# The seam between a routed and a dense mixture of experts: branch moved, shared block finished later

## The chip, the cores and the metric

The kernel runs on one core of a Trainium2 chip. The metric is device time in microseconds of one execution. Times inside a profile count from the first instruction of the profiled execution. TensorE (PE) multiplies, with its weight loads in a row of their own (PEld); VectorE (DVE), ScalarE (ACT) and GpSimd (POOL) do the rest, and SyncE (SP) issues most transfers.

## The reference

Three stages follow each other. Attention with rotated positions gives 1152 rows of 512 values. Each row then goes to one of 8 experts (`_moe_ref`), and the result goes through 8 experts that all work on all rows (`_moe2_ref`), weighted by a normalised gate:

```python
def _moe_ref(x, expert_emb, tau, w1, w2):
    ...
    expert_idx = np.argmax(logits, axis=1)
    ...
    for e in range(E):
        mask = expert_idx == e
        h = np.maximum(x[mask] @ w1[e], 0.0)
        out[mask] = gate_w[mask, None] * (h @ w2[e])

def _moe2_ref(x, w_gate, w1, w2):
    logits = x @ w_gate
    P = np.exp(logits - logits.max())
    for _ in range(8):
        P /= P.sum(1, keepdims=True) + 1e-09
        P /= P.sum(0, keepdims=True) + 1e-09
        P *= N / E
    for e in range(E):
        ye = np.maximum(x @ w1[e], 0.0) @ w2[e]
        out += P[:, e:e + 1] * ye
```

Sizes are N = 1152 rows, DM = 512, F = 1024 hidden values and E = 8.

## The kernel before

**Routed experts.** Rows are sorted into blocks of 128 rows of one expert. `run_blocks` works off NS = 10 blocks in a loop over i; iteration i holds the first layer of block i (`block_l1`) and the second layer of block i - 1 (`block_l2`). Weights come in 512 KB pieces into four raw buffers per layer (`fetch`, left out by a condition when the next block has the same expert) and are split by ScalarE and VectorE into a high and a low part (`split`). `block_in` gathers a block's rows from DRAM (xd); `block_out` scales the result by the gate and GpSimd scatters its rows to DRAM (yd) with an indirect transfer.

**The shared block.** Experts with few rows left over share one more block, number NB: four groups of 32 rows, each with its own expert's weights. `place_quad` finds its rows, `quad_tokens` turns them, `quad_product(s)` for s = 0 to 3 is a quarter of its first layer, `quad_relu` and `quad_turn` follow, and s = 4 to 7 are quarters of its second layer. `quad_fetch(s)` loads the 2 MB of weights that product s needs. In the old kernel the eight products stand in iterations 3 to 9 and its rows are scattered like those of any block.

**The branch.** Data may need more than 10 blocks. `rest_of_blocks` does those, behind a branch on a count that every engine reads for itself (`tc.If`, line 1009). With the data timed here it is not taken. Its not-taken side lets each queue wait for its own outstanding work.

**Dense experts.** `dense_experts` is a generator that is stepped from `run_blocks` for its first weights (`fetch1`, `prep_plain`). Behind the branch it loads yd in four quarters of 288 rows (line 1188), turns them on TensorE (`turn_quarter`, with warming products on a weight tile ahead), splits them into high and low parts (`split_quarter`) and starts the products (`plain`), the gate's normalisation (`sinkhorn`) and then the steady loop of `l1` and `l2`.

TensorE, VectorE, ScalarE and GpSimd run in the order in which the code is written. SyncE's order is made by a scheduler; each engine works its queue in order.

Of the kernel before, what the change touches and what calls it, by code (L numbers as in the profile page):

```python
# [49 lines left out]
def fused_kernel(ctx, tc, qk, vv, tab, cst, emb, tau, w1a, w2a, wg, w1b, w2b, out):  # L50
# [37 lines left out]

    mctx = ExitStack()
    rt = mctx.enter_context(tc.tile_pool(name="rt", bufs=1))  # L90
    cs = rt.tile([128, C_END], F32, name="cs")
    uo = rt.tile([128, 256], BF16, name="uo")
    rt.tile([128, 8], F32, name="pad")

    raw1p, raw2p = ([rt.tile([128, 2, F], F32, name=f"raw{m}{i}") for i in range(2)] for m in (1, 2))
# [400 lines left out]
    def squares(b):  # L496
        for c in range(NQ):
            sq = tmp("sq", [QT, DM], BF16) if (b, c) == (0, 0) else ops["sq"]
            ops["sq"] = sq
            yield A.activation(sq, ops["x", b][:, c], AF.Square, accum_out=nsq[:, b, c:c + 1])  # L500

    gv = tmp("gv", [QT, 3, B, NQ, NB], BF16)
# [43 lines left out]
    def quad_slots():  # L546

        z = tmp("z", [QT, E])
        V.tensor_scalar(z, grp, float(GS), 1024.0, op0=ALU.mult, op1=ALU.add)
        V.scalar_tensor_tensor(z, inq, -1024.0, z, op0=ALU.mult, op1=ALU.add)  # L550
        V.tensor_tensor(ws, ohb[:, :, :NQ], z.unsqueeze(1).unsqueeze(1).to_broadcast([QT, B, NQ, E]), op=ALU.mult)
        V.tensor_reduce(blk, ws, axis=AX.X, op=ALU.add)
        V.tensor_tensor(blk, blk, rk, op=ALU.add)
        sl = [QT, B * NQ, BLK]
        V.tensor_tensor(slot.rearrange("p b t n -> p (b t) n"), over(col("iota"), 1, sl),
                        over(blk.rearrange("p b t -> p (b t)"), 2, sl), op=ALU.is_equal)
# [236 lines left out]

    def block_out(i, p):
        y = mp.tile([BLK, DM], F32, tag="y", bufs=2, name="y")
        A.activation(y, p, AF.Copy, scale=gate[:, i:i + 1])
        G.indirect_dma_start(out=yd, out_offset=bass.IndirectOffsetOnAxis(ap=idx[:, 1, i:i + 1], axis=0),
# [10 lines left out]
    def quad_fetch(s):  # L808
# [5 lines left out]
        for r in quad["reg"]:  # L814
            w = early.tile([128, F], F32, tag="w", bufs=8, name="qw")
# [43 lines left out]
    def rest_of_blocks():  # L859

        own = [nc.sync.value_load(bei[0:1, i:i + 1], min_val=0, max_val=E - 1) for i in range(NS, NB)]
        for n, i in enumerate(range(NS, NB)):
# [6 lines left out]
            x = mp.tile([128, F], F32, tag="qx", bufs=1, name="ex")  # L869
# [6 lines left out]
            h = block_relu(p)  # L876
            t = mp.tile([128, F], F32, tag="qx", bufs=1, name="eh")
# [5 lines left out]
            p = bank("y", 2, "y")  # L883
# [3 lines left out]
            block_out(i, p)  # L887

    def run_blocks(lo, hi, xb=None, w1=None, w2=None):

        def expert(i, raws, src, n):
            while len(reg) <= i < hi:
                reg.append(nc.sync.value_load(bei[0:1, len(reg):len(reg) + 1], min_val=0, max_val=E - 1))
            if 0 < i < hi:
                fetch(raws, src, n, reg[i], reg[i] != reg[i - 1])

        xb = xb or [block_in(i) for i in range(lo, min(lo + 2, hi))]
        if lo > 0:
            expert(lo, raw1, w1a, 128)
            expert(lo, raw2, w2a, 256)  # L900
        with tc.manual_schedule(engines=ORDERED):
            if w1 is None:
                *_, w1 = split(raw1p)
            expert(lo + 1, raw1, w1a, 128)
            if lo == 0:
                warm(w1[0][0], WARM)
            x = block_x(xb[0])
            if lo == 0:
                warm(w1[0][0], 3)
                split_low(raw2p[0], *w2[0])  # L910
            h = None
            for i in range(lo, hi + 1):
                begin, here, more = i == 0, i < hi, i + 1 < hi
# [10 lines left out]
                if i == 6:  # L924
                    quad_relu()
                elif i == 9:
                    block_out(NB, quad["p", 0])
                    tc.mark_branch_hint_location("rest", "LikelyTaken")
                if begin:
# [14 lines left out]
                if i in (6, 7):  # L944
                    quad_fetch(i - 1)
# [7 lines left out]
                if i + 2 < hi and len(xb) < i + 3 - lo:  # L953
# [3 lines left out]
                if more:  # L957
                    x = block_x(xb[i + 1 - lo])

                if i > lo:  # L960

                    turned = []
                    y = block_l2(h, w2, (lambda: turned.append(block_turn(hn))) if i == hi - 1 else None, i == hi)
                if i == 1:
                    place_rest(lambda: bank("x", 2, "gp"))
                    quad_slots()
                    quad_constants()
                elif i in (3, 4, 5, 7, 8):
                    quad_product({3: 0, 4: 1, 5: 2, 7: 5, 8: 6}[i])
                elif i == 6:  # L970
                    quad_turn()
# [3 lines left out]
                if i > lo:  # L975
                    block_out(i - 1, y)
                if here:
# [3 lines left out]
                    h = turned[0] if i == hi - 1 else block_turn(hn)  # L981
                if i in (1, 3, 4, 5, 7):
                    quad_fetch({1: 1, 3: 2, 4: 3, 5: 4, 7: 7}[i])
                for _ in range({7: 2, 9: 4}.get(i, 0)):
                    next(dense)

    reg = [0]
    with tc.manual_schedule(engines=ORDERED | {mybir.EngineType.SP}):
# [18 lines left out]
        dense = dense_experts(ctx, tc, early, yd, wgk, w1b, w2b, out, ident, ones)  # L1007
        run_blocks(0, NS, xb, pieces(first_w1), first_w2)
    with tc.If(nc.values_load(bei[0:1, NB:NB + 1], min_val=0, max_val=NB) > NS, label="rest"):
        rest_of_blocks()  # L1010
# [7 lines left out]
def dense_experts(ctx, tc, early, yd, wgk, w1b, w2b, out, ident, ones):  # L1018
# [124 lines left out]
    pp = ctx.enter_context(tc.tile_pool(name="pd", bufs=1, space=PSUM))  # L1143


# [33 lines left out]
    def htile():  # L1179

        return dp.tile([128, 2, 2, N], F32R, tag="h", bufs=2, name="h")

    gs = []
    for i in range(4):
        if i % 2 == 0:
            gt = dp.tile([128, 4 * N], F32, tag="h", bufs=2, name="g")
        g = gt[:TQ, i % 2 * 3 * DM:(i % 2 + 1) * 3 * DM].rearrange("p (t d) -> p t d", t=3)
        nc.sync.dma_start(out=g, in_=yd[i * QW:(i + 1) * QW].rearrange("(p t) d -> p t d", t=3))
        gs.append(g)
    for n in (2, 3):  # L1190
        fetch1(n)

    def turn_quarter(i, n):
# [3 lines left out]
        w = w1[0, 0]["t"][:, 0]  # L1197
        for _ in range(n):
            T.matmul(bank(d[0], 0), w[:, :128], w, start=True, stop=True)  # L1199
        for k in range(KD_):  # L1200
            for t in range(3):
                T.transpose(bank(d[k // 2], k % 2)[:, t:QW:3], gs[i][:, t, k * 128:(k + 1) * 128],  # L1202
                            ident[:TQ, :TQ])
        return d

# [105 lines left out]
    def plain(n, r, c, between=None):  # L1311
# [6 lines left out]
        for i, (a, y, k, wx, yx) in enumerate(todo):  # L1318
            if i and i % 3 == 0 and between:
                between(i)  # L1320
            for q in range(2):
                T.matmul(d[1][:, q, :QW], wv[:, wx, a, k], yq[yx][:, y, k, q * QW:(q + 1) * QW],  # L1322
                         start=(i == 0), stop=(i == len(todo) - 1))
# [27 lines left out]
    acc = dp.tile([128, N // 128, DM], F32, name="acc")  # L1351
# [194 lines left out]
```

## Time and profile before

| | |
|---|---|
| median of 3 runs | 1124.4 us (1123.49 to 1125.94) |
| the profiled execution | 1124.6 us, of which 1122.8 us lie between its first and last instruction (the span) |
| TensorE | busy 1095.6 us, 98% of the span |
| VectorE, ScalarE, GpSimd | 777.0, 467.6 and 130.6 us busy |
| mean granted clock of TensorE | 0.993 |
| chain of work that ended last | 67% TensorE, 1% VectorE in its named part |

In this execution attention ends around 172 us, the routed experts run to about 334 us, and the dense experts fill the rest. A busy TensorE in the profile is not one at its peak, since ends of products are modelled; what a stretch costs is read from the starts of what follows. "Idle before" in a row is the time in which the engine had nothing to do, with what ended it behind the arrow.

### The profile page before, as it was taken

To read this page: it belongs to the slowest core of one execution; us is meant where nothing else is said; L and a number is where in the kernel's file an instruction comes from. 1 tells how busy PE (TensorE), PEld (TensorE's weight loads), DVE (VectorE), ACT (ScalarE), POOL (GpSimd) and SP (SyncE) were. 2 spreads that over 40 slices of the span, in tenths; PEclk is the share of its full clock that TensorE was granted. 3 is DMA by queue.
4 is the path that set the end of the run, shared out by engine and by line. 5 is a ranking of instruction groups with operands and counts; after the bars stand their busy time and mean duration, and the time that the engine had idled before them with its cause. 6 is when DMAs were issued, how large, how long until landed. Compare 5 with 4: busy or idle time off the path is not lost.

```text
span 1122.8 us, 16884 instructions
## 1 busy us (share of the span) xinstructions
PE 1095.6 (98%) x6605; PEld 928.4 (83%) x6606; DVE 777.0 (69%) x1257; ACT 467.6 (42%) x742; POOL 130.6 (12%) x106
## 2 busy tenths in 40 slices
PE   8999996999989999999999999999999999999998
PEld 4777775777768989988988989899988989888987
DVE  6767768976753697867766667666676666766665
ACT  4656746776853433333333333223333233333330
POOL 7674403232220000000000000000000000000000
PEclk9999998999998999999999999999999999999999
DMA  8688713657725011111111111111111111111002
GB/s 243 181 226 261 183 28 128 244 198 262 242 90 159 22 60 52 38 38 54 41 57 38 39 40 55 57 39 38 38 58 53 41 38 39 57 40 55 20 1 85
DMA packets 74980, 102.09 MB, mean 91 GB/s; under 512 B 5128, under 2 KB 46600, under 8 KB 74128
## 3 DMA queue, kind: packets, MB, share of 16 engines
q1 hardware_dynamic: 72528, 94.12, 27.2%
q0 software_dynamic: 1760, 5.77, 1.4%
q8 instruction: 54, 0.88, 0.3%
q10 hardware_dynamic: 608, 1.07, 0.3%
q14 instruction: 30, 0.25, 0.1%
HBM read 110.31 MB, written 7.60 MB: 105 GB/s over the span
## 4 chain that ended last, share of the span: by engine, by line
PE 67%; DVE 1%; DMA 0%; issue 0%; SPq 0%
PE o L1359 35%; PE d L1305 29%; PE d L1322 2%; DMA g<-yd 0%; DVE acc L1365 0%; PE d L1202 0%; PE o L1249 0%; PE d L1199 0%; DVE h L1347 0%; DVE w L1071 0%; DVE w L1132 0%; PE o L1202 0%; DVE acc L1370 0%; DVE P L1284 0%; DVE rs L1273 0%
## 5 line engine op out<-in xcount | busy, mean ns | idle before, releaser
L1359 PE MATMUL o<-w,h 128*128 128x512 f32 x1728 | 435.6, 394 | 0.4 <-DVE acc L1365 0.4
L1305 PEld LDWEIGHTS d<-yq,w 128*128 128x128 f32 x2520 | 355.6, 188 | 17.9
L1305 PE MATMUL d<-yq,w 128*128 128x288 f32 x2520 | 367.3, 294 | 0.0
L1359 PEld LDWEIGHTS o<-w,h 128*128 128x128 f32 x1728 | 312.1, 188 | 57.8 <-DVE acc L1365 0.7
L1370 DVE SCALAR_TENSOR_TENSOR acc<-o,P,acc 128x512 f32<-128x512 f32 x252 | 189.1, 751 | 160.9 <-PE o L1359 160.9
L1346 ACT ACTIVATE h<-st 128x576 fp32r<-128x576 f32 x90 | 61.7, 685 | 217.3 <-DVE st L1336 217.3
L1333 ACT ACTIVATE st<-d 128x576 f32<-128x576 f32 x90 | 58.7, 652 | 219.3 <-PE d L1305 219.3
L725 DVE TENSOR_TENSOR wlo<-raw,whi 128x2048 fp32r<-128x2048 f32 x40 | 91.0, 2288 | 24.8 <-ACT whi L732 24.6
L1336 DVE TENSOR_TENSOR st<-st,d 128x576 f32<-128x576 f32 x90 | 67.6, 751 | 39.4 <-PE d L1305 39.4
L249 DVE TENSOR_REDUCE nb<-s 120x1 f32<-120x576 f32 (+1 forms) x80 | 60.3, 754 | 37.4 <-PE s L243 24.1
L1070 ACT ACTIVATE w<-raw 128x512 fp32r<-128x512 f32 x124 | 70.8, 574 | 19.6 <-DVE raw L1115 16.0
L255 ACT ACTIVATE p<-s,nb 120x576 f32<-120x576 f32 (+1 forms) x80 | 59.0, 737 | 47.0 <-DVE nb L249 44.6
L1071 DVE TENSOR_TENSOR w<-raw,w 128x512 fp32r<-128x512 f32 x124 | 76.5, 619 | 0.0
L732 ACT ACTIVATE whi<-raw 128x2048 fp32r<-128x2048 f32 x36 | 69.0, 1916 | 15.8 <-PE h L760 7.2
L1347 DVE SCALAR_TENSOR_TENSOR h<-st,h 128x576 fp32r<-128x576 f32 x90 | 67.5, 750 | 0.4 <-ACT h L1346 0.3
L243 PE MATMUL s<-kd,qd 128*120 128x288 f32 x280 | 54.5, 317 | 1.2 <-ACT p L255 1.2
L243 PEld LDWEIGHTS s<-kd,qd 128*120 128x120 f32 x280 | 38.5, 178 | 14.0 <-ACT ph L281 5.7
L300 PE MATMUL o<-ph,vr 120*64 120x288 f32 x320 | 46.8, 417 | 0.0
L283 DVE COPY ph<-pt 120x480 f32<-120x480 f32 x64 | 41.4, 648 | 2.1 <-PE pt L277 2.1
L1347 DVE SCALAR_TENSOR_TENSOR h<-d,h 128x576 fp32r<-128x576 f32 x38 | 28.7, 756 | 19.4 <-ACT h L1346 19.4
L1132 DVE TENSOR_TENSOR w<-raw,w 128x1024 fp32r<-128x1024 f32 x32 | 39.0, 1218 | 0.4 <-ACT w L1131 0.4
L277 PE MATMUL pt<-io,p 120*120 120x120 f32 x256 | 37.0, 267 | 1.2 <-DVE ph L283 1.2
(285 smaller groups left out, 1046.5 us busy)
## 6 DMA issues: line engine op xcount, KB each, us to landing
raw<-w1a SPq DMA_DIRECT2D x40, 512.0 KB
raw<-w2a SPq DMA_DIRECT2D x40, 512.0 KB
raw<-w1b SPq DMA_DIRECT2D x64, 256.0 KB
raw<-w2b SPq DMA_DIRECT2D x32, 512.0 KB
qw<-w1a SPq DMA_DIRECT2D x16, 512.0 KB
qw<-w2a SPq DMA_DIRECT2D x16, 512.0 KB
kd<-hl SPq DMA_DIRECT2D x28, 288.0 KB
r<-qk SPq DMA_DIRECT2D x6, 1152.0 KB
```

What stands on the lines that cost most here:

```text
L243: T.matmul(s[:m, h, :HS], qd[:, j, t * QT:t * QT + m], kd[:, j, x, h * HS:(h + 1) * HS], start=(x == 0), stop=(x == 1))
L249: V.tensor_reduce(nb[:m], s[:m, :, :HS], axis=AX.XY, op=ALU.max, negate=True)
L725: V.tensor_tensor(lo, raw, hi, op=ALU.subtract)
L732: A.activation(hi, raw, AF.Copy)
L1070: A.activation(hi, src, Copy)
L1071: V.tensor_tensor(lo, src, hi, op=ALU.subtract)
L1305: T.matmul(d[1][:, q, :QW], wv[:, wx, which, k], yq[yx][:, YQ[p], k, q * QW:(q + 1) * QW], start=new and k == 0 and (wx, yx) == (0, 0), st ...
L1336: V.tensor_tensor(halves(st[x]), halves(st[x]), mid(d), op=ALU.add)
L1346: A.activation(hi, src, AF.Relu)
L1347: V.scalar_tensor_tensor(lo, src, 0.0, hi, op0=ALU.max, op1=ALU.subtract)
L1359: T.matmul(d, hs[n][:, r, hx, t * 128:(t + 1) * 128], w2[n][:, wx, r], start=(r == 0 and (hx, wx) == (0, 0)), stop=(r == 1 and hx == 1))
L1370: V.scalar_tensor_tensor(a, d, p, a, op0=ALU.mult, op1=ALU.add)
```

## The change

- The buffers `raw1` and `raw2` and the constants `cs` move into two large tiles (`areas`) that last into the dense stage; the quarters of yd are loaded into them, and small tiles (`sq`, `gv`) and the shared block's result (`y_quad`) lie in their ends.
- The shared block's one-hot rows (`quad_slots`) are made in steps in iterations 1 to 3; its placing moves from iteration 2 to 4, its products 0 to 3 to iterations 5 to 7, and products 4 to 7 behind the last block. Weights of products 6 and 7 go into buffers of split weights.
- Its rows are no longer scattered. `no_rows` scatters zeros to them at iteration 5; at the seam `quad_places` makes a matrix with a one where a row of the shared block belongs, and `add_quad` adds the rows, in a high and a low part, to the turned quarters in PSUM.
- The branch moves to iteration NS - 2, behind the second layer of block 7. `rest_of_blocks` loads block 8's second-layer weights again at its end.
- Of 39 warming products 4 stay. The loads of the third and fourth dense weights are issued behind the quarters of yd. `plain` without work in between takes one half of the columns after the other.

```diff
+    areas = [hp.tile([128, 4 * N], F32, tag="h", bufs=2, name="raw") for _ in range(2)]
+    raw1p, raw2p = ([a[:, i * 2 * F:(i + 1) * 2 * F].rearrange("p (x f) -> p x f", x=2) for i in range(2)] for a in areas)
+    y_quad, cs = areas[0][:, 4 * F:4 * F + DM], areas[1][:, 4 * F:4 * F + C_END]
+    quarters = [areas[i // 2][:TQ, i % 2 * 2 * F:][:, :3 * DM].rearrange("p (t d) -> p t d", t=3) for i in range(4)]
...
-        V.tensor_tensor(slot.rearrange("p b t n -> p (b t) n"), over(col("iota"), 1, sl),
-                        over(blk.rearrange("p b t -> p (b t)"), 2, sl), op=ALU.is_equal)
+        for b in range(B):
+            yield
+            sl = [QT, NQ, BLK]
+            V.tensor_tensor(slot[:, b], over(col("iota"), 1, sl), over(blk[:, b], 2, sl), op=ALU.is_equal)
+        yield
...
+    def no_rows(i):
+        y = mp.tile([BLK, DM], F32, tag="y", bufs=2, name="y")
+        G.memset(y, 0.0)
+        scatter(i, y)
...
-                if i == 2:
-                    place_quad(lambda: bank("q", 2, "qp"))
+                if i == 4:
+                    place_quad(quad_bank)
                     quad["xb"] = block_in(NB)
-                elif i == 3:
+                elif i == 5:
                     quad_tokens()
-                elif i in (6, 7, 9):
-                    quad_product({6: 3, 7: 4, 9: 7}[i])
...
-                elif i in (3, 4, 5, 7, 8):
-                    quad_product({3: 0, 4: 1, 5: 2, 7: 5, 8: 6}[i])
+                elif i in (5, 6, 7):
+                    quad_product({5: 0, 6: 1, 7: 3}[i])
+                    if i == 7:
+                        quad_relu()
+                if i == NS - 2:
+                    with tc.If(nc.values_load(bei[0:1, NB:NB + 1], min_val=0, max_val=NB) > NS, label="rest"):
+                        rest_of_blocks(reg[i])
...
+                if i in (1, 5, 6, 7, 8):
+                    quad_fetch({1: 1, 5: 2, 6: 3, 7: 4, 8: 5}[i])
+                elif i == 9:
+                    quad_fetch(6)
+                    quad_fetch(7)
...
+            quad_product(4)
+            quad_product(5)
+            for _ in range(4):
+                next(dense)
+            quad_product(6)
+            quad_product(7)
+            half = DM // 2
+            A.activation(y_quad[:, :half], quad["p", 0][:, :half], AF.Copy, scale=gate[:, NB:])
+            V.tensor_scalar_mul(y_quad[:, half:], quad["p", 0][:, half:], gate[:, NB:])
...
-    with tc.If(nc.values_load(bei[0:1, NB:NB + 1], min_val=0, max_val=NB) > NS, label="rest"):
-        rest_of_blocks()
...
+    with tc.issue_after(load.ins):
+        for n in (2, 3):
+            fetch1(n)
+
+    def quad_places():
+        nt = N // 128
+        V.tensor_copy(near[:, nt:nt + 1], idx_quad)
+        V.tensor_scalar(near[:, :nt], iota[:, :nt], -128.0, near[:, nt:nt + 1], op0=ALU.mult, op1=ALU.add)
+        sh = [128, nt, 128]
+        V.tensor_tensor(there.rearrange("p (t n) -> p t n", t=nt), iota.unsqueeze(1).to_broadcast(sh),
+                        near[:, :nt].unsqueeze(2).to_broadcast(sh), op=ALU.is_equal)
+
+    def quad_parts():
+        A.activation(y_parts[0], y_quad, Copy)
+        V.tensor_tensor(y_parts[1], y_quad, y_parts[0], op=ALU.subtract)
...
+    def add_quad(i, d):
+        for k in range(KD_):
+            for y in y_parts:
+                T.matmul(bank(d[k // 2], k % 2)[:, :QW], y[:, k * 128:(k + 1) * 128], there[:, i * QW:(i + 1) * QW],
+                         start=False, stop=(y is y_parts[1]), skip_group_check=True)
...
-        hs[0] = htile()
-        d = [turn_quarter(0, 28), turn_quarter(1, 6)]
+        quad_places()
+        quad_parts()
+        d = [turn_quarter(0, 4), turn_quarter(1)]
+        for i in range(2):
+            add_quad(i, d[i])
         split_quarter(0, d[0])
-        d.append(turn_quarter(2, 5))
+        d.append(turn_quarter(2))
         split_quarter(1, d[1])
+        add_quad(2, d[2])
         c11 = plain(0, 0, 0)
         split_quarter(2, d[2])
-        d.append(turn_quarter(3, 0))
+        d.append(turn_quarter(3))
+        add_quad(3, d[3])
         c21 = plain(0, 1, 0)
+        hs[0] = htile()
```

Where instructions stand, in program order. On TensorE the branch of the old kernel comes behind the last product of the last block; y is the second layer, wlo the low part of its weights:

```order
L790 MATMUL y<-whi,hl__3479 128x512
L790 MATMUL y<-whi,hh 128x512
L790 MATMUL y<-whi,hl__3479 128x512
L790 MATMUL y<-wlo,hh 128x512 [waits DVE_49]
L790 MATMUL y<-wlo,hh 128x512 x3
L1009 TENSOR_LOAD bei [waits DVE_49]
L1009 COMPARE_AND_BRANCH
```

In the new kernel the rows in front of the branch are the last products of block 7's second layer:

```order
L794 MATMUL y<-wlo,hh 128x512
L794 MATMUL y<-whi,hl__3237 128x512
L794 MATMUL y<-whi,hh 128x512
L794 MATMUL y<-wlo,hh 128x512
L794 MATMUL y<-whi,hl__3237 128x512
L979 TENSOR_LOAD bei [waits DVE_49]
L979 COMPARE_AND_BRANCH
```

What follows the branch (the rows of its taken side left out) was, in the old kernel, the warming (d<-w) and turning (d<-io,g) of the dense stage:

```order
L1009 UNCONDITIONAL_BRANCH
L1009 UNCONDITIONAL_BRANCH [waits PE_49]
L1199 MATMUL d<-w 128x512 [waits PE_49,Activation_49]
L1199 MATMUL d<-w 128x512 x27
L1202 MATMUL d<-io,g 128x96 [waits DMAHW7_49]
L1202 MATMUL d<-io,g 128x96 x11
L1199 MATMUL d<-w 128x512 x6
L1202 MATMUL d<-io,g 128x96 [waits DMAHW0_49]
```

The branch has moved from the end of the blocks to a place two blocks earlier. The seam itself, directly behind the shared block's last product, reads on TensorE in the new kernel (d<-w are the last three of the four warming products, io,raw the turning of a quarter, quad the one-hot matrix and the shared block's parts):

```order
L1233 MATMUL d<-w 128x512 x3
L1242 MATMUL d<-io,raw 128x96 [waits DMAHW3_49]
L1242 MATMUL d<-io,raw 128x96 x5
L1242 MATMUL d<-io,raw 128x96 [waits PE_49]
L1242 MATMUL d<-io,raw 128x96 x5
L1242 MATMUL d<-io,raw 128x96 [waits DMAHW4_49]
L1242 MATMUL d<-io,raw 128x96 x5
L1242 MATMUL o<-io,raw 128x96 [waits DVE_49]
L1242 MATMUL o<-io,raw 128x96 x5
L1249 MATMUL d<-quad 128x288 [waits Activation_49]
L1249 MATMUL d<-quad 128x288 [waits DVE_49]
L1249 MATMUL d<-quad 128x288 x10
```

Two quarters are turned one after the other and the one-hot products follow them, where the old kernel had the branch, 28 warming products and six more between the quarters. SyncE, behind its branch, asked for the quarters of yd in the old kernel so:

```order
L1009 UNCONDITIONAL_BRANCH
L1009 UNCONDITIONAL_BRANCH [waits SP_sequencer_49,DMAHW0_49,DMAHW1_49,DMAHW2_49,DMAHW3_49,DMAHW4_49,DMAHW5_49,DMAHW6_49,DMAHW7_49]
L1188 DMA g<-yd 96x1536 [waits DMASW5_49,DMAHW7_49,DMASW1_49,PE_49]
L1188 DMA g<-yd 96x1536 [waits DMAHW0_49]
L1188 DMA g<-yd 96x1536 [waits DMASW4_49,DMASW6_49,DMASW3_49,DMASW7_49,DMASW2_49,DMAHW1_49,DMASW0_49,PE_49]
L1188 DMA g<-yd 96x1536 [waits DMAHW2_49]
```

and in the new one, where the branch stands far ahead, behind the last weights of the shared block (qw):

```order
L838 DMA qw_3866<-w2a 128x2x512 [waits DMAHW1_49]
L838 ISA
L838 DMA qw_3866<-w2a 128x2x512 [waits DMAHW2_49]
L1212 DMA raw<-yd 96x1536 [waits DMAHW3_49,DMASW5_49]
L1212 DMA raw<-yd 96x1536 [waits DMAHW4_49]
L1212 DMA raw<-yd 96x1536 [waits DMAHW5_49,DVE_49]
L1212 DMA raw<-yd 96x1536 [waits DMAHW6_49,DVE_49]
L1105 DMA raw_3968<-w1b 128x4x128 [waits DMAHW7_49,DVE_49]
L1105 DMA raw_3968<-w1b 128x4x128 [waits DMAHW0_49]
L1105 DMA raw_3971<-w1b 128x4x128 [waits DMAHW1_49,DVE_49]
L1105 DMA raw_3971<-w1b 128x4x128 [waits DMAHW2_49]
```

The loads of dense weights (w1b) that stood ahead of SyncE's branch now stand behind the quarters of yd.

## Rows read from the trace of the kernel before

**Rows 1.** The page, 40 slices: TensorE's granted clock in tenths.

```profile
PEclk9999998999998999999999999999999999999999
```

**Rows 2.** Windows of one us: length, busy time by engine, PEclk, DMA share, GB/s.

```profile
335.00:336.00 1.00, 0.00 (x0) 0.00 (x0) 0.00 (x0) 0.00 (x0) 0.73 (x1) 0.96 0.80 228
336.00:337.00 1.00, 0.08 (x1) 0.11 (x1) 0.00 (x0) 0.00 (x0) 0.00 (x0) 0.50 0.42 94
...
343.00:344.00 1.00, 1.00 (x6) 0.81 (x5) 0.00 (x0) 0.00 (x0) 0.00 (x0) 1.00 0.87 154
...
351.00:352.00 1.00, 1.00 (x7) 0.57 (x6) 1.00 (x3) 0.78 (x3) 0.00 (x0) 1.00 1.01 246
```

**Rows 3.** Order of time on TensorE at the seam: start, us, what, idle before.

```profile
332.54 1.17 PE L790 MATMUL y<-wlo,hh 128*128 128x512 f32 x4
336.92 9.38 PE L1199 MATMUL d<-w 128*128 128x512 f32 x28 [3.21 <-PEq L1009]
346.96 1.21 PE L1202 MATMUL d<-io,g 96*128 96x96 f32 x12 [0.67 <-DMA g<-yd]
...
360.26 2.82 PE L1249 MATMUL o<-yt,lw 128*32 128x384 f32 x52
```

**Rows 4.** The branch's line by engine queue: ns min/median/max, first and last start.

```profile
L1009 SPq EVENT_SEMAPHORE  x9: 17/17/17, 341.3 to 342.0; - x9
...
L1009 DVEq COMPARE_BRANCH  x1: 72/72/72, 332.9 to 332.9; - x1
L1009 PEldq COMPARE_BRANCH  x1: 3492/3492/3492, 333.1 to 333.1; - x1
```

**Rows 5.** Order of time on GpSimd and SyncE at the seam.

```profile
334.76 0.97 POOL L797 DMA_INDIRECT yd<-y,idx  x1 [4.28 <-ACT y L796]
...
333.69 4.00 SPq L1082 DMA_DIRECT2D raw<-w1b  x4
342.22 1.98 SPq L1188 DMA_DIRECT2D g<-yd  x4
```

**Rows 6.** The tile yd, 320 to 350 us, then the whole run: transfers.

```profile
DMA to landing us min/median/max: 3.1/3.4/3.6
...
DMA to landing us min/median/max: 3.1/4.1/8.3
```

**Rows 7.** Order of time on TensorE in the last blocks.

```profile
310.66 1.92 PE L841 MATMUL q<-qw,qh 128*32 128x512 f32 x16
312.51 1.09 PE L775 MATMUL ht<-io,h 128*128 128x128 f32 x8
...
323.78 1.03 PE L775 MATMUL ht<-io,h 128*128 128x128 f32 x8
...
327.39 0.47 PE L790 MATMUL y<-whi,hh 128*128 128x512 f32 x1
```

**Rows 8.** Order of time on TensorE and VectorE in iteration 2.

```profile
216.37 0.66 PE L747 MATMUL xt<-io,xb 128*128 128x128 f32 x4 [1.62 <-DVE hl__2458 L778]
...
209.81 1.49 DVE L555 TENSOR_TENSOR slot<-cs,blk 120x1280 bf16<-120x1280 f32 x1
```

**Rows 9.** TensorE's wait at 173, and windows there and at 192.

```profile
177.13 0.62 PE L476 MATMUL ip<-vals,slot 120*128 120x16 bf16 x10 [4.18 <-DVE vals L464]
...
176.00:176.50 0.50, 0.00 (x0) 0.00 (x0) 0.43 (x3) 0.47 (x3) 0.00 (x0) 0.50 0.00 0
...
192.00:193.00 1.00, 0.29 (x3) 0.29 (x4) 1.00 (x1) 1.00 (x3) 0.00 (x0) 1.00 0.04 16
```

**Rows 10.** Windows of five us: a stretch of block weights.

```profile
260.00:265.00 5.00, 5.00 (x30) 3.35 (x32) 4.07 (x3) 4.20 (x5) 0.04 (x1) 1.00 1.04 422
```

**Rows 11.** The chain of waits: start, us, what.

```profile
348.17 1.41 PE d L1199 x6
...
350.58 1.19 PE d L1199 x5
...
357.12 3.20 PE d L1322 x24
```

More of the change, by code (lines that the diff above doesn't have):

```diff
@@ L813, in quad_fetch @@
         quad["w", s] = []
-        for r in quad["reg"]:
-            w = early.tile([128, F], F32, tag="w", bufs=8, name="qw")
+        for g, r in enumerate(quad["reg"]):
+            if s < KD_ + 2:
+                w = early.tile([128, F], F32, tag="w", bufs=8, name="qw")
+            else:
+                if g % 2 == 0:
+                    two = mp.tile([128, 2, F], F32, tag=("whi", "wlo")[g // 2], bufs=4, name="qw2")
+                w = two[:, g % 2]
             ei = bass.ds(r, 1)
@@ L952, in run_blocks @@
                     quad_fetch(0)
[L953 removed]
+                if i + 2 < NS and len(xb) < i + 3:
                     xb.append(block_in(i + 2))
@@ L980, in run_blocks @@
                     expert(i + 1, raw2, w2a, 256)
[L981 to L984, printed above, removed]
-                    next(dense)
+                    h = turned[0] if i == NS - 1 else block_turn(hn)
+                if i in (1, 2, 3):
+                    next(slots_)
+                elif i == 5:
+                    no_rows(NB)
+                if i in (1, 5, 6, 7, 8):
[3 more added lines that the diff above has]
+                    quad_fetch(7)
+                if i in (7, 8):
+                    next(dense)
+            quad_product(4)
[7 more added lines that the diff above has]
+            V.tensor_scalar_mul(y_quad[:, half:], quad["p", 0][:, half:], gate[:, NB:])
     reg = [0]
@@ L1006, in fused_kernel @@
         early = ctx.enter_context(tc.tile_pool(name="early", bufs=1, side="right", reuse_waits="tile"))
[L1007 to L1010 removed]
+        dense = dense_experts(ctx, tc, early, yd, hp, quarters, y_quad, idx[:, 1, NB:], cs[:, COLS["iota"]],
+                              wgk, w1b, w2b, out, ident, ones)
+        run_blocks(xb, pieces(first_w1), first_w2)
     mctx.close()
@@ L1015, in fused_kernel, with dense_experts @@
         pass
-def dense_experts(ctx, tc, early, yd, wgk, w1b, w2b, out, ident, ones):
+def dense_experts(ctx, tc, early, yd, hp, gs, y_quad, idx_quad, iota, wgk, w1b, w2b, out, ident, ones):
     nc = tc.nc
@@ L1179, in htile @@
     def htile():
-        return dp.tile([128, 2, 2, N], F32R, tag="h", bufs=2, name="h")
-    gs = []
+        return hp.tile([128, 2, 2, N], F32R, tag="h", bufs=2, name="h")
     for i in range(4):
[L1185 to L1189, printed above, removed]
@@ L1190, in dense_experts @@
-    for n in (2, 3):
-        fetch1(n)
-    def turn_quarter(i, n):
-        d = [take(), take()]
+        load = nc.sync.dma_start(out=gs[i], in_=yd[i * QW:(i + 1) * QW].rearrange("(p t) d -> p t d", t=3))
+    with tc.issue_after(load.ins):
[8 more added lines that the diff above has]
+                        near[:, :nt].unsqueeze(2).to_broadcast(sh), op=ALU.is_equal)
@@ L1317, in plain @@
                 for wx, yx in ((0, 0), (0, 1), (1, 0))]
[L1318 to L1323, printed above, removed]
+        halves_ = [(0, 1)] if between else [(0,), (1,)]
+        for q_ in halves_:
+            for i, (a, y, k, wx, yx) in enumerate(todo):
+                if i and i % 3 == 0 and between:
+                    between(i)
+                for q in q_:
+                    T.matmul(d[1][:, q, :QW], wv[:, wx, a, k], yq[yx][:, y, k, q * QW:(q + 1) * QW],
+                             start=(i == 0), stop=(i == len(todo) - 1))
         w["left"] -= 2
```

94 lines of the change are left out of this document (45 added, 49 removed).

## The prediction

> **What bounds the kernel now.** I read the 40 slices of the page first. TensorE's granted clock falls in two slices only [rows 1]; the second is where the routed experts end and the dense ones begin. The one-microsecond stretches there show the reader an idle TensorE, a clock that falls to half at 336 (0.50, that is 1.2 of 2.4 GHz) and is back at 343 [rows 2]. The order of time on TensorE names the parts [rows 3]: the second layer of the last block ends at 332.54 + 1.17 = 333.71; after a stall of 3.21 us put down to the branch come 28 products that warm the engine; the first real work is the turning of the first quarter at 346.96, which waited for the rows of yd. So the seam costs 346.96 - 333.71 = 13.25 us, none of which is work that the reference needs.
>
> Why 13.25: ScalarE scales the last block's result and GpSimd issues its scatter at 334.76 [rows 5], and the scatters of this stretch landed 3.1 to 3.6 us after issue [rows 6], so the rows lie in DRAM at about 338.2. SyncE asks for them only at 342.22 [rows 5]. It had issued four loads of dense weights from 333.69 to 337.69 [rows 5], then met the branch, whose not-taken side waits for all of its transfers; its semaphore instructions begin at 341.3 [rows 4]. The first quarter landed at 346.92, 4.70 us after SyncE's request [rows 3, 5].
>
> From 208 to 334 TensorE is nearly gapless, and one eighth of the shared block takes 312.51 - 310.66 = 1.85 us of it [rows 7]. One gap is 1.62 us, up to 216.37, where TensorE waited for VectorE, which made the shared block's one-hot rows first [rows 8].
>
> **The change part by part.** I write T for the end of the last block's second layer, 333.71 now.
>
> Shared block moved. Four of its eight products go from before T to behind it: T comes 4 x 1.85 = 7.4 us earlier. TensorE is the engine that is full there, so this is a real shortening of the blocks; the four products lie in the seam, where there was nothing. Its turning and its placing only change blocks (0).
>
> One-hot rows of the shared block. They are now made in two halves behind the block's own work on VectorE, so the wait of 1.62 us should go [rows 8]; bounds 0 and -1.6, I take -1.6, since the operations named as releaser stand behind the moved ones, and the 1.49 us alone nearly fill the wait.
>
> Branch between two blocks. TensorE's compare took 3492 ns, VectorE's 72 [rows 4]; TensorE stood 3.21 us [rows 3]. Behind it now are the transposes of block 8 and block 9's first layer, so the whole stall is on the path: +3.2. The body that is jumped over has six blocks of 28 products in both kernels, so I expect the same stall; bounds 0 and 3.5. VectorE passes its own in 72 ns, the others jump over fewer instructions than TensorE, and all have slack of a microsecond and more per block beside TensorE; SyncE's wait for its transfers falls where its next request waits for VectorE anyway: 0.
>
> Clock behind the stall. After 333.71 the clock fell some 2.2 us later and stayed low to nearly 343, about 5.8 us past the end of the stall [rows 2, 3]; there it slowed only warming products. Now it would slow the blocks: 5.8 us at half speed are 2.9 us. The other bound is 0: in thin work at 192, with TensorE busy 0.29 of that microsecond, the clock stayed at 1.00 [rows 9]. The nearest row is the same stall, so I take +2.9.
>
> T becomes 333.7 - 7.4 - 1.6 + 3.2 + 2.9 = 330.8.
>
> Behind T. Scale and issue as now (334.76 - 333.71 = 1.05), 3.4 to land, 0.1 for SyncE, which now has no branch and no dense loads in front of the rows, then 4.70: the first quarter lands at T + 9.25; bounds T + 9.0 and, with the longest scatter of the whole run, 8.3 us [rows 6], T + 14.1. TensorE meanwhile has four products of the shared block (7.4 us) and four warming ones (0.9), so it waits about 1 us.
>
> Weights for those products: slices 6 and 7 (2 MB each) take the place of block 8's second-layer weights, so slice 6 can start when half of that layer is done and slice 7 when all is: 323.78 and about 327.4 in the old kernel, 9.9 and 6.3 us before T [rows 7]. At 422 GB/s [rows 10] 2 MB need 5 us, so both are there at about T + 2.7, and slice 7 is first read at T + 5.6. Not on the path.
>
> Rows from the first quarter to the end of the second dense product. Before: 360.26 - 346.92 = 13.3 us [rows 3]. Out go the warming products between the quarters, 1.41 + 1.19 = 2.6 us on the chain of waits [rows 11]. But the first six covered the second quarter: a quarter of 576 KB at 246 GB/s [rows 2] takes 2.4 us and turning one takes 1.0, so 1.4 us of waiting return. In come 4 quarters x 4 x 2 = 32 products of 288 columns; 24 such take 3.20 us [rows 11], so 32 x 0.133 = 4.3. Sum 13.3 - 2.6 + 1.4 + 4.3 = 16.4. The one-hot matrix (1152 columns) and the two parts of the shared result are made by VectorE and ScalarE while TensorE waits for rows (both have nothing else there): 0. The zeroed rows that GpSimd now scatters at block 5 stand on an engine that waited 4.28 us even for the last scatter [rows 5]: 0.
>
> End of that product: T + 9.25 + 16.4 = 330.8 + 25.65 = 356.5, against 360.3: 3.8 us earlier. Behind it both kernels run the same dense steps on a full TensorE, so the gain stays. Profiled execution: 1124.6 (span 1122.8) - 3.8 = 1120.8; the median of the runs shown is 0.2 lower than that execution, so 1120.6 to 1120.8. I predict 1120.8.
>
> **A rule of the skill.** Only TensorE's compare is long [rows 4]. The Trainium skill, "Runtime: NRT & Kernel Launch", Instruction fetch mechanics, says that code is fetched ahead in sequence, in blocks, and that a taken branch stalls when its target is not in the two blocks at hand. The trace agrees in that TensorE jumps over the most instructions; no row shows the blocks. By that rule the stall could also vanish, if the moved branch happens to lie where its target has been fetched: the first rival.
>
> **Rivals.**
> 1. No stall. For it: VectorE passes in 0.07 us [rows 4]. Against it: TensorE's jump is as long as before. Without stall there is no fall of the clock either: 3.2 + 2.9 more, 1124.6 - 9.9 = 1114.7.
> 2. Stall, but the clock holds. For it: the wait of 1.62 us left it alone, and the work around the gap is dense on both sides. Against it: the same 3.2 us brought it down, and so did the wait of 4.18 us up to 177.13 [rows 9]. 2.9 more: 1117.9.
> 3. The clock falls in the seam too. TensorE waits about 1 us before the first quarter, turns it in 1.0 and waits 1.4 again; that is thin work for 3.5 us, like the stretch at 192, which kept its clock, but with less in it. At 5.8 us of half speed, 2.9 are lost: 1123.7, no change.
> 4. Slower: the late weights. Slices 6 and 7 come when the rows of yd do. If their 4 MB move at 246 GB/s [rows 2] instead of 422, they need 17 us from about T - 7.9, end at T + 9, hold up the scatter (8.3 instead of 3.4 us to land) and then the quarters: the first lands at T + 14.1 instead of 9.25, 4.9 late, and TensorE's clock falls as well (2.9). 1120.8 + 7.8 = 1128.6. It decides from a first quarter at T + 13 on, where the gain is gone. For it: these loads are the only ones that were moved to the end; against it: the weight loads of the blocks ran at 400 GB/s and more.
>
> **How the numbers follow.** A measurement of this kernel tells about 0.2%, 2.2 us, from no change: faster is under 1122.2, slower over 1126.6. Forecast 45% (own range 1119 to 1123), rival 1 12%, rival 2 18%, rival 3 15%, rival 4 10%. Faster: most of the forecast (38), rivals 1 and 2 (30) and a little of 3: 0.69. No change: the rest of the forecast and most of 3: 0.21. Slower: rival 4, 0.10. The range runs from rival 1's edge to past rival 3: 1115.0 to 1125.0 leaves out rival 4 and a part of 1.
>
> **What would show it.** Right: a gap of about 3 us on TensorE in front of block 8's transposes, a clock of 0.50 behind it for some 6 us, no wait for VectorE around 214, the four late products directly behind the last block, SyncE's request for yd about 4.6 us after T, the first quarter at T + 9.3, 32 products of 288 columns in 4.3 us. Wrong: a first quarter past T + 11, waits of late products on DMA, or new waits for VectorE in blocks 2 to 4, which lose the 1.85 us of cover that their shared products gave.

## The result, and the profile after

The changed kernel takes 1136.39 us in the median of four runs (1134.17 to 1138.12), the kernel before 1124.32 on the same chip: a ratio of 1.0105 with an interval of 1.0082 to 1.0127. It is slower by 12 us, where 3.8 us less were predicted. In the profiled execution, the slowest of the four, the span grew from 1122.8 to 1136.3 us:

| place | before | predicted | after |
|---|---|---|---|
| T, end of the last block's second layer | 333.71 | 330.8 | 338.22 |
| first quarter turned from | T + 13.25 | T + 9.25 | T + 13.35 |
| from there to the end of the second dense product | 13.3 | 16.4 | 18.9 |
| from there to the end of the span | 762.5 | 762.5 | 765.8 |

TensorE's order of time after, at the branch and at the seam (start, us, what, idle before), to be compared with [rows 3, 7]. A name with q is an engine's queue of instructions; hh and hl are the high and low part of the hidden values:

```profile
308.59 0.39 PE L794 MATMUL y<-whi,hl__3237 128*128 128x512 f32 x1
311.88 1.06 PE L779 MATMUL ht<-io,h 128*128 128x128 f32 x8 [2.91 <-PEq L979]
...
321.83 0.80 PE L794 MATMUL y<-whi,hh 128*128 128x512 f32 x1 [3.41 <-ACT hh L781]
...
324.27 0.80 PE L794 MATMUL y<-whi,hl__3755 128*128 128x512 f32 x1 [1.22 <-DVE hl__3755 L782]
...
328.29 1.03 PE L779 MATMUL ht<-io,h 128*128 128x128 f32 x8
...
337.11 1.11 PE L794 MATMUL y<-wlo,hh 128*128 128x512 f32 x4
...
346.71 1.90 PE L858 MATMUL q<-qw,qh 128*32 128x512 f32 x10 [0.60 <-DMA qw<-w2a]
...
351.57 2.11 PE L1242 MATMUL d<-io,raw 96*128 96x96 f32 x12 [1.84 <-DMA raw<-yd]
...
370.49 2.82 PE L1295 MATMUL o<-yt,lw 128*32 128x384 f32 x52
```

The stall behind the branch is there, 2.91 us, but two waits follow that nobody forecast: for ScalarE's hh, 3.41, and for VectorE's hl, 1.22. ScalarE's order of time shows why:

```profile
307.46 0.61 ACT L754 ACTIVATE xh<-xt 128x512 fp32r<-128x512 f32 x1
...
317.00 1.92 ACT L736 ACTIVATE whi<-raw 128x2048 fp32r<-128x2048 f32 x1 [8.94 <-SPq L979]
318.82 0.67 ACT L805 ACTIVATE y<-y,gate 128x512 f32<-128x512 f32 x1
```

It stood for 8.94 us, until SyncE left its branch. The branch's line by engine queue, to be compared with [rows 4]:

```profile
L979 SPq EVENT_SEMAPHORE  x9: 17/17/17, 316.0 to 317.0; - x9
...
L979 PEldq COMPARE_BRANCH  x1: 6167/6167/6167, 305.3 to 305.3; - x1
...
L979 DVEq COMPARE_BRANCH  x1: 72/72/72, 308.7 to 308.7; - x1
L979 SPq TENSOR_LOAD <-bei x1: 274/274/274, 311.3 to 311.3; - x1
```

SyncE came to the branch last, at 311.3, and its not-taken side let go at 317.0. What it did until then and later stands in the order of time on its queue and on GpSimd (to be compared with [rows 5]):

```profile
302.97 2.34 SPq L838 DMA_DIRECT2D qw<-w2a  x4
305.35 5.90 SPq L1105 DMA_DIRECT2D raw<-w1b  x4
321.38 2.97 SPq L84 DMA_DIRECT2D raw<-w2a  x4
324.92 10.60 SPq L838 DMA_DIRECT2D qw<-w2a  x12
346.98 1.77 SPq L1212 DMA_DIRECT2D raw<-yd  x4
...
333.12 1.92 POOL L809 DMA_INDIRECT yd<-y,idx  x1 [11.03 <-ACT y L805]
341.30 0.99 POOL L809 DMA_INDIRECT yd<-y,idx  x1 [6.27 <-ACT w L1093]
```

Eight loads, 3 MB, stand between block 8's weights and the branch; they must be issued (to 311.25) and land. In the seam 12 late weight loads were issued to 335.5, and the last scatter starts only at 341.30, 3.1 us behind T. The row names ScalarE, but the scatter also waits for the one before it, which was issued at 333.12. The two took 7.5 and 5.7 us to land (yd's transfers from 335 to 375 us, to be compared with [rows 6]), to 340.6 and 347.0, and at 346.98 SyncE asks for the rows:

```profile
DMA to landing us min/median/max: 5.7/6.6/7.5
```

The clock, in windows of five us (columns as in [rows 2]), fell in TensorE's wait for ScalarE and again in the seam (to be compared with [rows 1, 2]):

```profile
315.00:320.00 5.00, 3.42 (x16) 2.49 (x14) 1.05 (x1) 3.00 (x3) 0.23 (x1) 1.00 0.03 6
320.00:325.00 5.00, 1.95 (x4) 1.14 (x5) 4.73 (x4) 3.18 (x4) 2.09 (x1) 0.60 0.14 52
325.00:330.00 5.00, 5.00 (x22) 4.10 (x21) 0.39 (x1) 1.02 (x3) 0.00 (x0) 0.72 0.75 248
335.00:340.00 5.00, 5.00 (x34) 2.83 (x36) 1.97 (x1) 0.69 (x1) 0.04 (x1) 1.00 1.04 393
...
350.00:355.00 5.00, 3.22 (x19) 2.93 (x20) 0.69 (x1) 0.31 (x1) 0.00 (x0) 0.67 1.01 256
355.00:360.00 5.00, 5.00 (x29) 4.68 (x27) 1.99 (x3) 2.57 (x6) 0.00 (x0) 0.65 1.10 259
```

### The profile page after: what moved, and what is told of

It reads as the page before. It is cut to its first block, busy times and chain, and to the rows that moved or that the text cites. A ratio compares the mean times of both kernels' runs of the same rounds, so it can differ in the third digit from the quotient of the medians.

```text
span 1136.3 us, 16887 instructions
## 1 busy us (share of the span) xinstructions
PE 1103.5 (97%) x6603; PEld 934.3 (82%) x6603; DVE 781.6 (69%) x1263; ACT 468.1 (41%) x743; POOL 134.4 (12%) x107
## 4 chain that ended last, share of the span: by engine, by line
PE 68%; DMA 2%; DVE 2%; ACT 0%; issue 0%; SPq 0%; DVEq 0%; ACTq 0%
PE o L1407 35%; PE d L1351 29%; PE d L1370 2%; DMA qw<-w2a 1%; PE y L794 1%; DMA raw<-yd 1%; DMA yd<-y,idx 0%; PE d L1249 0%; DVE acc L1413 0%; PE o L1295 0%; PE d L1242 0%; DVE wlo L729 0%; DVE h L1395 0%; ACT whi L736 0%; DVE w L1094 0%
```

## The experiments

My theory (A): the branch is a meeting point, SyncE comes last and holds ScalarE; and the late weights hold up the last scatters. The first rival (B): ScalarE's hold is its own, the price of its own jump. Others are named where they are tried. Each kernel was timed against the kernel before on the same chip; 0.1% is 1.1 us.

| kernel | median us | ratio to before, interval |
|---|---|---|
| changed, again | 1135.73 | 1.0083 (1.0067 to 1.0099) |
| SyncE's loads behind the branch | 1134.03 | 1.0068 (1.0055 to 1.0081) |
| no branch | 1126.74 | 1.0006 (0.9995 to 1.0018) |
| no late weights | 1130.42 | 1.0036 (1.0023 to 1.0049) |
| branch back at the end | 1127.63 | 1.0013 (1.0002 to 1.0024) |
| both paddings | 1131.83 | 1.0051 (1.0037 to 1.0065) |
| dense padding alone | 1134.90 | 1.0071 (1.0055 to 1.0087) |
| load order | 1124.90 | 0.9993 (0.9984 to 1.0002) |
| load order, paddings | 1122.35 | 0.9971 (0.9959 to 0.9982) |
| load order, paddings, warming | 1119.65 | 0.9947 (0.9934 to 0.9961) |
| before, rows asked for first | 1122.22 | 0.9976 (0.9963 to 0.9989) |

**SyncE's loads behind the branch.**

```diff
-                if i in (1, 5, 6, 7, 8):
-                    quad_fetch({1: 1, 5: 2, 6: 3, 7: 4, 8: 5}[i])
+                if i in (1, 5, 6):
+                    quad_fetch({1: 1, 5: 2, 6: 3}[i])
+                elif i == 8:
+                    quad_fetch(4)
+                    quad_fetch(5)
...
-                if i in (7, 8):
+                if i in (8, 9):
                     next(dense)
```

> The changed kernel with two groups of loads put behind the branch: the first dense weights (4 requests) and the fifth slice of the shared block (4 requests). Nothing is left out. Theory A: the branch is a meeting point. SyncE came to it last (at 311.9, out by 317.0, since it stood behind these loads), and ScalarE's first split behind the branch waited for it, 8.9 us, which cost TensorE 3.4 + 1.2 us. With the loads gone SyncE passes at about 308, ScalarE waits under 4 us, TensorE's waits for hh and hl go, and slices 4 and 5 land before block 9, so that the last scatters are less in the way of weights: 1136.4 - 4.6 - 3 = about 1129, and about 1126 if the clock then stays up. Theory B: ScalarE's hold is its own, the price of its own jump: nothing at the branch changes, and the time stays within 2 us of 1136.4.

SyncE's branch was at 302.4 and over at 305.5, ScalarE's wait 0.3 us instead of 8.9, TensorE's stall 0.59, and the last block ended at 328.29 instead of 338.22. That is theory A, and B falls. But the time fell by 0.15 to 0.37% only (against the changed kernel's two ratios), since the late products now waited for the weights that had been moved (TensorE's order of time):

```profile
334.89 1.05 PE L858 MATMUL q<-qw,qh 128*32 128x512 f32 x2 [3.03 <-DMA qw<-w2a]
...
346.91 3.25 PE L858 MATMUL q<-qw,qh 128*32 128x512 f32 x10 [2.22 <-DMA qw<-w2a]
```

The hold was cured, and most of its price paid again at the late products; my 1129 left that out. Nor is the branch a meeting of all engines: in the changed kernel TensorE worked behind it from 311.88 on, 5.1 us ahead of SyncE's release at 317.0. Held is what waits for SyncE.

**No branch.** The `tc.If` in iteration NS - 2 is taken out.

> The changed kernel without the branch and its body (blocks beyond ten are left out; the data has none). Theory A: the branch costs TensorE's jump (2.9), ScalarE's hold through SyncE (3.4 + 1.2), and the clock that falls behind it (2.6), 10.1 in all, and some of the late weights' delay, which SyncE's hold made worse: 1123 to 1126.5. Theory B: only the jump and the clock belong to the branch, 5.5: 1131. Both: if the loss lies in the first block and the dense stage instead, 1133 and more.

The last block ended at 326.1 and the ratio fell to 1.0006, by 9 to 11 us: A's 10.1, not B's 5.5. The rest of the change comes out even with the kernel before. SyncE's loads stand in the same order as in the changed kernel, and ScalarE's split at this place started at 304.89 without a wait, so it is not the loads by themselves that held it. The seam is no shorter without the branch (order of time on TensorE and SyncE):

```profile
333.54 1.90 PE L858 MATMUL q<-qw,qh 128*32 128x512 f32 x10 [0.99 <-DMA qw<-w2a]
...
338.96 1.21 PE L1238 MATMUL d<-io,raw 96*128 96x96 f32 x12 [2.39 <-DMA raw<-yd]
...
312.67 9.43 SPq L838 DMA_DIRECT2D qw<-w2a  x12
```

The last late weights came at T + 7.4, the first quarter at T + 12.9.

**No late weights.**

```diff
-                    quad_fetch(6)
-                    quad_fetch(7)
+                    for s in (6, 7):
+                        quad["w", s] = [w[0].bitcast(F32) for w in w2]
```

> The changed kernel without the loads of the shared block's slices 6 and 7 (4 MB); their products read weights of the last block that lie in SBUF, so the shared block's result is another one. Theory A: these loads filled the transfer engines until 344 and held up the last two scatters (7.5 and 5.7 us to land instead of 3.4): without them the first quarter comes about T + 9.3 instead of T + 13.4 and two waits of 0.8 us go: about 1132. Theory C: the scatter was late for another reason (GpSimd, ScalarE's order): T + 13 stays and the time is within 1 us of 1136.4.

T was 338.59 here; order of time on TensorE, GpSimd and SyncE:

```profile
347.47 0.71 PE L1242 MATMUL d<-io,raw 96*128 96x96 f32 x6 [0.75 <-DMA raw<-yd]
...
339.64 0.96 POOL L809 DMA_INDIRECT yd<-y,idx  x1 [4.29 <-ACT y L805]
...
342.37 1.94 SPq L1212 DMA_DIRECT2D raw<-yd  x4
```

The scatter starts 1.05 us behind T, the rows are asked for 2.7 us later, and the first quarter comes at T + 8.9 instead of T + 13.35: theory A. The branch's hold is there as before (ScalarE 9.8 us), so the two losses are separate.

**Branch back at the end.** The `tc.If` stands ahead of `quad_product(4)`, without the load at the end of its body.

> The changed kernel with the branch put back behind the last block, ahead of the shared block's four late products (the load that its body would repeat is left out with it); the data takes no branch in either. Theory A: no hold of ScalarE and no stall inside the blocks, so the last block ends near 326.5 as without the branch; behind it TensorE has the jump again, 3.2 us, and SyncE asks for the rows only when the late weights have landed and its branch is passed; the rows then come about 3 us later than without branch: 1128 to 1130, so that 7 us of the loss belong to the branch's move and not to the shared block's. Rival: with the late weights in flight the jump takes 6 us and all engines meet there, so that the seam costs as much as the branch between the blocks did: 1134 to 1137.

A on the total, the rival on the jump: at the end TensorE stood 5.66 us, but 3.4 of it lie where TensorE waited for weights and rows without a branch. The clock fell behind this jump, was back at 1.00 from 340 on, and stayed up while the quarters were turned: from the first quarter to the end of the second dense product 15.8 us passed, against 18.9 without a branch. Moving the branch between the blocks costs 8 to 10 us, the rest of the change 1.5. In the order of time the last scatter names its predecessor here.

```profile
L998 PEldq COMPARE_BRANCH  x1: 6112/6112/6112, 326.5 to 326.5; - x1
...
  PE q L858: 5.7, 1
```

```profile
330.09 0.97 POOL L809 DMA_INDIRECT yd<-y,idx  x1 [6.20 <-DMA yd<-y,idx]
```

**Paddings.** In the dense loop the mean time from the start of a group of 12 products of 288 columns to the next group was 1.584 us in the two kernels of the old layout and 1.593 in all of the new one. yq, which these products read, had moved by an odd multiple of 64 bytes.

```diff
     uo = rt.tile([128, 256], BF16, name="uo")
+    rt.tile([128, 16], F32, name="pad")
...
-    near = dp.tile([128, 16], F32, name="near")
+    near = dp.tile([128, 32], F32, name="near")
```

> The changed kernel with two paddings and nothing else: 64 bytes in front of the dense operands (yq, which stood at an odd multiple of 64 bytes in the partition, at an even one in the kernel before), and 64 bytes in front of attention's buffers (r, kd, qd, in the same way). Theory D: the new addresses make the 288 column products of the dense stage slower (a group of 12 took 1.593 us in all four kernels of the new layout and 1.584 in both of the old) and the loads of attention's keys later (attention ended 1.1 to 1.8 us later): the group falls to 1.584, attention's end to 161.7, and the time by about 4 us, to 1132.4. Rival: the 0.6% and the wait at 45 us belong to other things that moved (hidden values, the accumulator, the constants in one tile with the weights): 1136 stays. If only one of the two falls, the time is 2.7 or 1.3 us lower.

> The changed kernel with the first of the two paddings alone, the 64 bytes in front of the dense operands. Theory D: the groups of 12 products take 1.583 us and the time falls by 2.7 us, 0.24%. If attention's padding had a part in the 6 us that both together gave, this is 3 us over that; if it had none, this one is the same as both, and the rest of the 6 us lies in how the clock happened to fall.

With the second padding the group takes 1.583 us in all four kernels that have it, without it 1.593 in all seven. Over 200 groups of the dense loop, the first and last row in TensorE's order of time, without padding (load order) and with it:

```profile
426.83 1.64 PE L1409 MATMUL o<-w,h 128*128 128x512 f32 x6
...
1103.49 11.83 PE L1409 MATMUL o<-w,h 128*128 128x512 f32 x50
```

```profile
426.37 1.64 PE L1410 MATMUL o<-w,h 128*128 128x512 f32 x6
...
1100.92 2.25 PE L1410 MATMUL o<-w,h 128*128 128x512 f32 x9
```

676.66 against 674.55 us: 2.1 us by 64 bytes, where theory D had 2.7. This half of it is shown in the groups. The attention half is not: with its padding attention's last row began at 162.9, 161.5 and 163.1, without it in the new layout at 162.5 to 163.5, and in the old at 161.7. What delays it stays open. In times, the dense padding alone gave 0.12% with overlapping intervals; both gave 3.6 to 6 us on the changed kernel, of which only these 2.1 are explained, and 2.5 us on the one with the load order.

**Changed again.** The same kernel.

> The changed kernel itself, once more, beside the next two on one chip. All theories: 1.0 to 1.1% over the kernel before. Its second trace tells what of the early losses (attention ending 1.5 us later, 2.4 us more in the first block with a clock that fell at 194) comes from the change and what varies between executions: if they come from the change, both are there again; if not, the first block takes 16 us as before.

1.0083, its interval overlapping with the first one's. Hold (9.2 us), stall (3.65) and late scatter (341.36) are there again; the first quarter came at T + 11.8. Attention ended 1.2 us later than in the kernel before; in the first trace it was 1.5. The first block's wait of 2.47 us at 195 is not there again:

```profile
194.03 0.66 PE L779 MATMUL ht<-io,h 128*128 128x128 f32 x4 [1.60 <-ACT h L770]
```

The block took 17.5 us, against 18.9 in the first trace and 16.45 before. In eight of the other nine kernels of the new layout it took 15.6 to 16.4 us, so this part of the early loss varies between executions. The clock behind the stall was another one too (order of time on TensorE, and a window of five us):

```profile
311.15 1.34 PE L779 MATMUL ht<-io,h 128*128 128x128 f32 x8 [3.65 <-PEq L979]
312.14 1.20 PE L764 MATMUL h<-whi,xh 128*128 128x512 f32 x2
...
310.00:315.00 5.00, 3.85 (x15) 3.31 (x16) 0.00 (x0) 0.00 (x0) 0.00 (x0) 0.68 0.65 167
```

It fell here directly behind the stall, as forecast (the two rows took 1.06 and 0.71 us in the first trace), and again in TensorE's wait for ScalarE.

**Load order, then paddings, then warming.** Three cures, added one by one. In the first the edit moves the first dense weights by one iteration, from 7 to 6, not by two.

```diff
                     if i == 7:
                         quad_relu()
+                        quad_fetch(4)
...
                         rest_of_blocks(reg[i])
+                    quad_fetch(5)
...
-                if i in (1, 5, 6, 7, 8):
-                    quad_fetch({1: 1, 5: 2, 6: 3, 7: 4, 8: 5}[i])
+                if i in (1, 5, 6):
+                    quad_fetch({1: 1, 5: 2, 6: 3}[i])
...
-                if i in (7, 8):
+                if i in (6, 8):
                     next(dense)
```

> The changed kernel with three groups of loads in another place and nothing left out: the first dense weights two iterations earlier, the fifth slice of the shared block ahead of block 8's second-layer weights instead of behind them, the sixth directly behind the branch. Theory A: SyncE passes its branch as early as in the run with these loads behind it (305.5), ScalarE is not held (9 us less), and the late products don't wait for weights, as they did there (5.9 us); what remains of the late weights is slices 6 and 7. The last block ends near 328, the second dense product near 358: about 1126. Theory B': with these loads ahead the transfer engines are busy at the branch, TensorE's jump is as long as in the changed kernel (6.2 us) and SyncE leaves late: 1132.

> Both edits before this one together. If they are independent, their gains add up: about 1126 - 4 = 1122, a little under the kernel before. If the alignment is nothing, 1126.

```diff
-        d = [turn_quarter(0, 4), turn_quarter(1)]
+        d = [turn_quarter(0, 12), turn_quarter(1, 5)]
```

> The kernel with both edits, and in the seam 12 instead of 4 warming products ahead of the first quarter and 5 ahead of the second. Theory E: the clock falls in the seam since TensorE waits there (about 2.4 us of the 18.9 from the first quarter to the second dense product are the low clock; 15.9 were seen where the clock had not fallen before it), and products that fill the waits keep it up: 2 to 2.5 us less than without, about 1120. Rival: the turning itself is thin enough for the clock to fall, or the products delay the quarters: no gain, or 1 us more.

The first and the third came out as A and E said; of the 4 us that D promised 2.5 came. The branch's line with the new load order, SyncE in time and TensorE's jump short:

```profile
L980 SPq EVENT_SEMAPHORE  x9: 17/17/17, 304.4 to 305.0; - x9
...
L980 PEldq COMPARE_BRANCH  x1: 3627/3627/3627, 303.5 to 303.5; - x1
...
  ACT whi L736: 0.3, 1
  PE ht L779: 0.3, 1
```

The clock in the seam without the warming products (load order alone) and with them, 340 to 345 us:

```profile
340.00:345.00 5.00, 4.33 (x22) 4.33 (x23) 0.41 (x1) 0.79 (x2) 0.00 (x0) 0.50 1.00 230
```

```profile
340.00:345.00 5.00, 4.35 (x38) 3.96 (x36) 3.30 (x6) 3.48 (x7) 0.00 (x0) 1.00 1.09 256
```

From the first quarter to the end of the second dense product 19.0 us (18.9 with the paddings) became 17.2. That is 1.7 of the 2.7 us of this last step; 1.1 us more lie in rows that came earlier, at T + 10.4 instead of T + 11.5, which the warming products don't explain. The last of these kernels is the best of all, 0.53% under the kernel before.

**The kernel before, rows asked for first.** The third and fourth dense weights under `tc.issue_after` the quarters, 12 warming products instead of 28.

> The kernel before, in which only the third and fourth dense weights are asked for behind the quarters of yd, and of the 28 warming products 12 stay, since they would cover the gain. Theory A: in the old seam SyncE's four requests in front of the branch delayed the rows by 4 us; now it waits at its branch early, asks for the rows when the last scatter has landed (about 338.3 instead of 342.2), the first quarter lands near 343 and the gain is 3 to 4 us: about 1121. Rival: with fewer warming products the clock is low while the quarters are turned, which gives 2 us back: about 1123. Third: SyncE's wait at the branch holds the rows whatever stands ahead of it: 1124.

SyncE was through its branch at 320.6 and asked for the rows 5.0 us behind the last block's end instead of 8.5; the first quarter came 9.6 us behind it instead of 13.25. So the seam's reading was right: four loads ahead of the branch, for which SyncE waited there, cost 3.6 us, of which 2.7 (0.24%) show in the time.

## Why the prediction was wrong

- **Shared block moved (-7.4) and the wait of 1.62 (-1.6): right.** Without the branch the last block ends at 326.1, with attention 1.1 us later than before: 325.0 against 324.7 by these two terms. No wait for VectorE is left around 214.
- **Stall (+3.2): the sum right by luck.** It was 2.91 (3.65 in the second trace), but not since the jump is the same: the compare took 6.17 us instead of 3.49, and TensorE's queue was 3.7 us ahead of the multiplying array instead of 0.6, so that a longer jump was hidden to a longer part. With the load order cured the jump takes 3.63 us and 0.3 of it shows.
- **"SyncE's wait for its transfers falls where its next request waits for VectorE anyway: 0": this step failed.** I asked who waits for SyncE's next request, not who waits for SyncE. ScalarE's first split behind the branch waits for it, 8.9 us, and TensorE lost 3.41 + 1.22 by that. The same step has "all have slack of a microsecond and more per block": ScalarE had, but a few us and not nine.
- **Clock (+2.9): size right, place right in one trace of two.** In the profiled execution twelve products from 321.83 to 328.29 took 6.46 - 1.22 = 5.2 us where 12 x 0.228 = 2.7 is full speed (neighbouring starts at 308.36 and 308.59 are 0.23 apart): 2.5 us. It fell 9 us behind the stall, in the wait for ScalarE, and not behind the stall itself, which is rival 2. In the second trace it fell behind the stall too (the transposes and the first layer of block 9 took 8.15 us instead of 6.5) and then in the wait, and with both paddings a stall of 2.92 us brought it down (0.51 from 312 to 314). So stalls of 2.91 and 2.92 us went either way, and forecast and rival 2 could not be told apart beforehand. Where 0.3 us of the stall and no wait were left, it stayed at 1.00 to the seam.
- **First quarter at T + 9.25 with slices 6 and 7 not on the path: failed.** T + 13.35 here and T + 11.8 in the second trace, on either side of T + 13, the point of decision of rival 4, which named T + 14.1 and this mechanism and had 10%. The last scatter was issued at T + 3.1 and not at T + 1.05, since the one before it took 7.5 us to land; from there to SyncE's request 5.7 us passed instead of 3.5, and from the request to the first quarter 4.6 instead of 4.7. Without these loads T + 8.9. I had the weights done at T + 2.7 (starts at T - 9.9 and T - 6.3 and 5 us for each slice give T + 0.1) and left out slice 5: twelve loads stand in this queue and not eight. SyncE's hold is not the reason: without a branch the first quarter came at T + 12.9 too, and with slice 5 loaded earlier at T + 10.4 to T + 11.5.
- **Rows to second product (16.4): right for a clock that stays up** (15.8 with SyncE's loads behind the branch and with the branch at the end, 17.2 with 13 more warming products), short by 2.5 where it falls. Rival 3 had this fall by itself and rival 4 beside its late rows; the forecast had it at nothing.
- **Behind it "both kernels run the same dense steps": failed by 3.3 us**, 2.1 of them the 64 bytes. That the buffers move was in front of me, and I took the speed of a product to be independent of it. The other 1.2 us stay open.

The sum for the profiled execution: T is 338.22 - 330.8 = 7.4 us late (4.6 ScalarE's hold, 4.2 in attention and the first block, part of it varying between executions, the rest smaller with either sign), 4.1 in the seam, 2.5 in the turning, 3.3 in the dense loop: 17.3 against the forecast span of 1119.0 (15.6 between the medians, 1136.4 and 1120.8).

## What to carry to other kernels

A branch between two steps couples engines: price it by the engine that arrives last, with everything its queue has in front of it (transfers in flight included), ask what behind the branch waits for that engine, and keep that queue empty there. Moved loads keep their bytes: when a request or a wait is moved, look for the stretch in which the same bytes must now pass, and for the small urgent transfer that will stand behind them. When buffers move, compare the cadence of one unchanged group of products in both traces before anything else.

## What the runs showed of the hardware

TensorE's code itself comes over the transfer engines. In the changed kernel and in the one with the load order, the queues of a stretch around TensorE's compare (queue, kind: packets, MB, share):

```profile
q1 hardware_dynamic: 102, 0.20, 103.5%
q8 instruction: 1, 0.02, 11.9%
```

```profile
q8 instruction: 1, 0.02, 15.1%
```

The rows don't name the engine of the packet; in each of the twelve traces with a branch exactly one on this queue lies inside TensorE's compare, 2.2 to 2.9 us ahead of its end. The first is 308.9 to 309.4, 3.6 us behind the compare's start at 305.3, in the middle of weights; the second 304.4 to 304.9, about 1 us behind it, alone. In both the compare ends about 2.4 us after this packet, as in the kernel before (packet at 334.1, end 336.6). The jump took 3.4 to 3.9 us in the six traces in which the transfer engines' mean busy share during it was 0.02 to 0.35, and 6.1 to 6.9 us in the six in which that share was 0.97 to 1.06. The Trainium skill, "Runtime: NRT & Kernel Launch", Instruction fetch mechanics, says that each sequencer drives a transfer queue of its own for its code and that a taken branch outside the fetched blocks forces such a transfer; the packets agree (the branch taken is here the jump over the unused body). That the packet comes later among data, and by how much, these traces show; that it stands behind the data is the likely reason. What of the jump reaches TensorE's work is the jump less the queue's lead over the array: 6.1 - 0.6 with the branch at the end (5.66 measured), 3.6 - 3.7 with the load order (0.3).

A product of 288 columns takes 0.6% longer in the seven traces in which yq, its operand of 288 columns, starts at an odd multiple of 64 bytes in the partition by the program's addresses; its weights stand at the same place in all. The tiles behind yq, the second layer's weights among them, move with it, and which of them does it was not separated.
